# Carrying a decay from the free axis to the partitions: through device memory by DMA instead of by products with ones

## Chip, cores and metric

One core of a Trainium2 chip runs the kernel. The metric is the device time in microseconds of one execution, from the median of several runs. The engines are TensorE (PE, with PEld for its weight loads), VectorE (DVE), ScalarE (ACT), GpSimd (POOL) and SyncE (SP); each works off its own queue in order, and waits on semaphores for the others. Sixteen DMA engines move data for all of them.

## The reference

A gated linear attention over 768 steps, for 4 batches and 8 heads of 48 dimensions, and behind it a two-layer network with a squared ReLU on all 3072 tokens (384 to 2048 to 384):

```python
for t in range(S):                                  # S = 768
    state = alpha[:, :, t, :, None] * state + np.einsum('bhd,bhe->bhde', k[:, :, t], v[:, :, t])
    y[:, :, t] = np.einsum('bhd,bhde->bhe', q[:, :, t], state)
x = y.transpose(0, 2, 1, 3).reshape(B * S, H * D)   # 3072 x 384
h = x @ w_in                                        # 384 x 2048
out = np.maximum(h, 0.0) ** 2 @ w_out               # 2048 x 384
```

Inputs and output are float32; alpha lies between 0.8 and 1, and has one value for each step, head and dimension of k.

## The kernel before

The work is cut into 12 units of 256 tokens, numbered g = 0 to 11: first the four batches' first thirds (0 to 3), then their second (4 to 7), then their last (8 to 11). So unit g + 4 goes on with the state that unit g left. Two tokens lie in one partition (256 tokens on 128 partitions, axis j of size 2).

For each unit these steps follow each other; the names are those of the orders further down:

- load: alpha, k, q, v into RAW (lda, ldk, ldq, ldv). Most go through SP's queue; unit 2's and the weights (win0, win1, wout0, wout1) go through POOL's. Unit 3's alpha is issued only when wout0 has landed (AFTER).
- front: decays. For units 2 to 11 (decays_by_pair) the two tokens of a partition are multiplied (pr, on DVE or POOL), a logarithm is taken (ln, ScalarE), and a product with a triangular matrix of ones sums the logarithms over the partitions (m1i, PE, into psW, L684). Exponentials of it, by ScalarE, give the factors for k (ei, L695, tile EK) and for q (ea, L697, tile EQ). The last row of EQ[:, 1] holds each dimension's total decay over the unit.
- The total decay is needed once more, to multiply the state (sd). The state has its k dimensions on the partitions, two heads at a time: tile SBD is 128 x 384. So the total has to stand as a column over the partitions. The kernel before makes it with four more products of PE, of the logarithms as weights with a 128 x 2 matrix of ones (L687, part of m1i), and ScalarE's exponential of these eight columns into ACM (ec, L700). Units 0 and 1 do the like in functions of their own; units 8 to 11 need none, as nothing follows them.
- scaling of q and k (ekm, eqm on DVE), transposes (tr: by PE for units 0 to 2, by DMA through SP's queue from unit 3), scores (p), mask (mk, tile pm), output (y, which takes the state product of the next unit with it), state (sa, sc, sd on DVE or POOL).
- the network: xe and xt bring the unit's output into the layout for PE, s1 is the first layer in 8 groups, re the ReLU, sq the square, s2 the second layer in 8 groups, oe the copy out of PSUM and out the store.

Every operation is recorded by Program.add with what it reads and writes. Program.schedule then orders all engines' queues ahead of the run, with costs, priorities and a table of shifts written into the program; Program.fill puts products with zeros (L1143, name "fill") into PE's idle time ahead of the first s1; Program.place sets the waits, Program.emit writes the queues. The order in which an engine takes its operations is thus fixed. Two parts of it matter here. POOL's queue, from the weights on, is

    wout0 wout1 sd1 pr3 sd2 vc4 pr5 vc5 pr6 vc7 vc10

and PE's, around unit 3's decays, is

    kv2 m1i3 s2_0_1_0 s2_0_1_1 s2_0_1_2 s2_0_1_3 m1s3 y2

(vc is the cast of v, kv a state product, m1s3 a second product with a triangular matrix, s2_0_1_x the second layer of unit 0.) A tile with a number that repeats is one of a few buffers: EQ, EK and ACM have two, by g % 2.

Of the kernel before, what the change touches and what calls it, by code (L numbers as in the profile page):

```python
# [2 lines left out]

# [3 lines left out]
ALU = mybir.AluOpType  # L7
# [7 lines left out]
class Op:  # L15


    __slots__ = ("alts", "eng", "fn", "cost", "prio", "deps", "idx", "lag", "sem", "start", "end", "pos", "name",
                 "users", "ndeps", "mode", "ready", "land")

    def __init__(self, alts, prio, name):
        self.alts, self.prio, self.name = alts, prio, name
        self.eng = self.fn = self.cost = None
        self.deps = {}
        self.lag = 0
        self.sem = None
        self.users = []
        self.pos = None
        self.mode = ("F", "F")
        self.ready = 0.0  # L30
        self.start = self.end = self.land = None


class Program:

    HOP = 35
    PE_LATENCY = 170
    DMA_FIRST = {"sp": 1300, "act": 1300, "pool": 2000}  # L40
    PACKET = (("win", 172), ("wout", 490), ("ld", 22), ("tr", 18), ("xt", 18), ("out", 125))
    SBUF_ONLY = ("pr", "bk", "aq", "ekm", "eqm", "sq", "sb", "sd")
    BIAS = {"pool": 300}
    DMA_LAST = {"sp": 800, "act": 800, "pool": 1900}
    SWITCH = 95
    HALVED = {"qks": 3, "kqt": 3, "raw": 3, "ek": 3, "eq": 3, "acm": 2, "laf": 2}
    AFFINITY = 2500

    SHIFT = {
# [55 lines left out]
    }  # L105

# [1068 lines left out]
```

## Time and profile before

| | |
|---|---|
| device time, three runs | 174.98, 174.0 and 175.28 us; median 174.98 |
| span of the profiled execution | 174.5 us, 5094 instructions, mean granted TensorE clock 1.000 |
| busy in the span | PE 169.1 us, DVE 121.3, ACT 117.6, POOL 18.8 |
| DMA | 33.36 MB in 74743 packets; queue q1 (SP's) 71.4% of the sixteen engines' span, q0 (POOL's) 12.1% |

The profile is of one execution. Its span, from the first instruction to the last, is 174.5 us; the page gives no other time for that execution, so sums are made against this span, and the runs' median is 0.5 us above it. Lines as L687 are those of the kernel before. An engine that is called busy for 97% need not work at its best: matmuls overlap, and their ends are modelled. A wait has the name of what ended it. "q0" and "q1" are the queues through which POOL's and SP's transfers go; one transfer is split over the DMA engines, and the program counts 16 steps of a semaphore for its landing.

### The profile page before, as it was taken

Reading aid. Unit: us, or ns where it says so; the run is one execution under the profiler, and the core shown is the slowest. Engines: PE = TensorE matmul, PEld = TensorE weight load, DVE = VectorE, ACT = ScalarE, POOL = GpSimd, SP = SyncE. Lnnn points to the kernel's source line nnn. Section 1 sums busy time; section 2 is a strip of 40 time slices with the busy share of each in tenths; the row PEclk is TensorE's granted clock in tenths of the full one; section 3 lists DMA queues with packets and bytes.
Section 4 is the critical chain, followed back from the end, with each engine's and each line's share of the span. In section 5 each row is a group of like instructions: output and inputs, shape, how many; then the busy total and the mean of one; then the engine's idle time right before and its main releaser. Section 6 shows DMA issues by size and latency. Waiting matters only on the chain.

```text
span 174.5 us, 5094 instructions
## 1 busy us (share of the span) xinstructions
PE 169.1 (97%) x2237; PEld 130.5 (75%) x2237; DVE 121.3 (70%) x197; ACT 117.6 (67%) x211; POOL 18.8 (11%) x28
## 2 busy tenths in 40 slices
PE   7989999999999999999999999999999999999994
PEld 2556898856886697777788886778788697688773
DVE  5497799797967869866778966868849726322230
ACT  3848698868869569768768757378668564566440
POOL 3159010022102120000100000000200000000000
DMA  5999999979998999798998897999899690040022
GB/s 139 324 297 190 274 303 216 230 208 280 274 229 125 274 235 188 200 222 151 278 212 211 228 196 180 275 201 251 201 214 208 115 196 4 0 135 4 10 80 90
DMA packets 74743, 33.36 MB, mean 191 GB/s; under 512 B 71649, under 2 KB 71905, under 8 KB 74721
## 3 DMA queue, kind: packets, MB, share of 16 engines
q1 hardware_dynamic: 73184, 28.32, 71.4%
q0 software_dynamic: 1536, 4.72, 12.1%
q8 instruction: 17, 0.28, 0.7%
q14 instruction: 6, 0.04, 0.1%
HBM read 25.17 MB, written 4.72 MB: 171 GB/s over the span
## 4 chain that ended last, share of the span: by engine, by line
PE 56%; DMA 26%; ACT 6%; DVE 4%; SPq 3%; POOL 2%; issue 1%
PE psO L1089 22%; PE psWH L1042 22%; DMA raw<-in_v_dram 9%; DMA wout<-in_moe_w_out_dram 8%; DMA raw<-in_alpha_dram 5%; DMA raw<-in_q_dram 5%; SPq L568 3%; PE psO L1143 2%; POOL raw L568 2%; ACT rr L1050 2%; PE psX L843 2%; PE psX L1012 2%; ACT vbf L742 1%; PE psZ L811 1%; PE psX L832 1%; PE psX L940 1%
## 5 line engine op out<-in xcount | busy, mean ns | idle before, releaser
L1042 PE MATMUL psWH<-xt,win 128*128 128x256 bf16 x576 | 73.9, 275 | 0.5 <-ACT rr L1050 0.2
L1042 PEld LDWEIGHTS psWH<-xt,win 128*128 128x128 bf16 x576 | 65.0, 145 | 6.2 <-DVE rr L1052 1.6
L1089 PE MATMUL psO<-wout,gt 128*128 128x384 bf16 x368 | 68.9, 326 | 0.0
L1050 ACT ACTIVATE rr<-psWH 128x512 bf16<-128x512 f32 x83 | 48.9, 596 | 21.5 <-PE psWH L1042 20.0
L1089 PEld LDWEIGHTS psO<-wout,gt 128*128 128x128 bf16 x368 | 34.8, 98 | 18.3 <-DVE gt L1060 0.2
L1060 DVE TENSOR_TENSOR gt<-rr 128x1024 bf16<-128x1024 bf16 (+1 forms) x47 | 28.4, 608 | 25.1 <-ACT rr L1050 24.5
L951 DVE TENSOR_TENSOR pm<-psX,caus 128x1024 bf16<-128x1024 f32 x12 | 14.6, 1220 | 2.4 <-PE psZ L940 2.1
L951 DVE TENSOR_TENSOR pm<-psZ,caus 128x1024 bf16<-128x1024 f32 x12 | 14.6, 1216 | 1.5 <-PE psZ L940 1.4
L1097 ACT ACTIVATE osb<-psO 128x384 f32<-128x384 f32 x19 | 9.3, 489 | 6.8 <-PE psO L1089 6.3
L971 ACT ACTIVATE xbf<-psX 128x768 bf16<-128x768 f32 x12 | 9.7, 806 | 5.0 <-PE psX L832 4.1
L746 DVE TENSOR_TENSOR qks<-raw,eq 128x384 bf16<-128x384 f32 x18 | 10.3, 605 | 3.0 <-DMA raw<-in_q_dram 3.0
L1143 PE MATMUL psO<-zero 128*128 128x512 bf16 (+1 forms) x37 | 10.5, 417 | 1.3 <-DVE zero L489 1.3
L741 POOL CAST vbf<-raw 128x768 bf16<-128x768 f32 x4 | 3.7, 930 | 71.5 <-DMA raw<-in_v_dram 71.5
L1064 ACT ACTIVATE gt<-rr 128x512 bf16<-128x512 bf16 (+1 forms) x13 | 10.8, 828 | 0.4
L751 DVE TENSOR_TENSOR qks<-raw,ek 128x768 bf16<-128x768 f32 x11 | 10.7, 969 | 0.4 <-ACT ek L663 0.3
L1052 DVE TENSOR_SCALAR rr<-psWH 128x512 bf16<-128x512 f32 x13 | 8.9, 687 | 2.0 <-PE psWH L1042 1.6
L742 ACT ACTIVATE vbf<-raw 128x768 bf16<-128x768 f32 x7 | 5.9, 845 | 3.5 <-DMA raw<-in_v_dram 3.5
L717 ACT ACTIVATE la<-raw 128x384 f32<-128x384 f32 x8 | 4.2, 523 | 5.3 <-DMA raw<-in_alpha_dram 5.2
L1143 PEld LDWEIGHTS psO<-zero 128*128 128x128 bf16 x37 | 3.5, 108 | 4.6 <-issue 1.9
L906 DVE TENSOR_TENSOR smd<-psZ,sbd 128x384 bf16<-128x384 f32 x8 | 4.4, 554 | 3.4 <-PE psX L832 3.4
L675 DVE TENSOR_TENSOR prd<-raw 128x384 f32<-128x384 f32 x7 | 4.0, 569 | 2.9 <-DMA raw<-in_alpha_dram 2.9
L678 ACT ACTIVATE lab<-prd 128x384 bf16<-128x384 f32 x10 | 5.2, 520 | 1.1 <-POOL prd L677 0.6
(115 smaller groups left out, 165.9 us busy)
## 6 DMA issues: line engine op xcount, KB each, us to landing
raw<-in_alpha_dram SPq DMA_DIRECT2D x11, 384.0 KB, 4.2
raw<-in_k_dram SPq DMA_DIRECT2D x11, 384.0 KB, 5.1
raw<-in_q_dram SPq DMA_DIRECT2D x11, 384.0 KB, 4.2
raw<-in_v_dram SPq DMA_DIRECT2D x11, 384.0 KB, 4.8
out_dram<-osb SPq DMA_DIRECT2D x11, 384.0 KB, 4.3
win<-in_moe_w_in_dram POOLq DMA_DIRECT2D x2, 768.0 KB, 9.9
wout<-in_moe_w_out_dram POOLq DMA_DIRECT2D x2, 768.0 KB, 15.2
raw<-in_alpha_dram POOLq DMA_DIRECT2D x1, 384.0 KB, 9.7
```

Of the source, the lines that this page charges most:

```text
L746: add("dve", lambda e, j=j, dst=dst: e.tensor_tensor(dst, RAW[r][:, 2, :, j, :].rearrange("p (n x) d -> p n x d", x=2), EQ[la][:, j].rearr ...
L751: add("dve", lambda e, a=a, E=E: e.tensor_tensor(QKS[qs][:, a, :, :, 0:D], RAW[r][:, 1 + a].rearrange("p h j d -> p j h d"), E[la][:].rear ...
L951: add("dve", lambda e, hf=hf, psT=psT: e.tensor_tensor(PM[pm][:, hf].rearrange("p r n j t -> p (r n) (j t)"), psT[:, :, :].rearrange("p r ...
L971: add("act", lambda e: e.activation(XBF[x2][:], psX[:, :, 0:HD], AF.Copy), act_ns(2 * HD), p0 + 6100, reads=[("ps", "X", 0), ("ps", "X", 1 ...
L1042: ins = pe.matmul(psH[hb][:, i * T:(i + 1) * T], WIN[:, kk, hidden(fj)], mov, start=(kk == 0), stop=(kk == KT - 1))
L1050: add("act", lambda e, hb=hb, rr=rr: e.activation(rr, psH[hb], AF.Relu), act_ns(512), pu + 600, reads=[("ps", "H", hb)], writes=[("rr", rb ...
L1052: alts={"dve": (lambda e, hb=hb, rr=rr: e.tensor_scalar(rr, psH[hb], 0.0, None, ALU.max), dve_ns(512))})
L1060: add("dve", lambda e, dst=dst, sq=sq: e.tensor_tensor(dst, sq, sq, ALU.mult), 148 + k * 267, pu + 1200, reads=[("rr", rb, h) for h in ran ...
L1064: "act": (lambda e, dst=dst, sq=sq: e.activation(dst, sq, AF.Square), act_ns(k * 512))})
L1089: ins = pe.matmul(psS, GT[gt][:, fj, j, :], WOUT[:, fj, :], start=(fj * parts % FT == 0), stop=((fj + 1) * parts % FT == 0))
L1097: add("act", lambda e, j=j, psS=psS: e.activation(OSB[ob][:, j], psS, AF.Copy), act_ns(DM), ps_ + 700, reads=[keyS], writes=[("osb", ob, j ...
L1143: pr.fill(lambda n: lambda pe: pe.matmul(psO[:, 0:n], ZERO[:, 0:128], ZERO[:, 0:n], skip_group_check=True), ((512, 216, 420), (256, 109, 2 ...
```

## The change

For units 2 to 7 (TOTALS_BY_DMA) the four products with ones and ScalarE's ec are left out. In their place POOL issues two transfers for each unit: et writes the last row of EQ[:, 1] (8 heads of 48 numbers) to a small tensor in device memory, LINE, in rows of 64; ec reads LINE back, one number at a time, so that two heads' rows become one column of 128 partitions, four columns in all (512 single float32 numbers, into ACM[:, 0:4]). ec waits until et has landed. LINE's columns 48 to 63 must be zero, so two transfers (zline0, zline1) first write zeros from a new tile NIL; et waits for them. sd multiplies by four columns, each spread over 96, where it took eight, each spread over 48.

The orders of the queues are written as tables, and stand as the planner before had put them, apart from what the change adds or takes: POOL's queue is now

    wout0 wout1 zline0 zline1 sd1 et2 ec2 pr3 et3 ec3 sd2 vc4 et4 ec4 pr5 et5 ec5 vc5 pr6 et6 ec6 et7 ec7 vc7 vc10

DVE has one fill more (znil) among the first, and sd3 stands five operations later, behind bk4 lb4 ekm4 eqm1_4 eqm0_4. SP's queue is the same, and so are the 37 products with zeros. With the tables, place also leaves out an engine's wait for itself where two of its operations only read the same bank of PSUM (ScalarE's ea behind ei, ec behind ea).

```diff
+    TOTALS_BY_DMA = (2, 3, 4, 5, 6, 7)
+    NIL = nc.alloc_sbuf_tensor("nil", [H, 64], FP32)
+    add("dve", fill(NIL[:], 0.0), 100, -2e6, writes=[("nil",)], name="znil")
...
-                if incl and not last:
+                if incl and not last and g not in TOTALS_BY_DMA:
                     for p in range(NPR):
                         ins = pe.matmul(psW[:, HD + 2 * p:HD + 2 * p + 2],
                                         LAB[la][:, 2 * p:2 * p + 2, :].rearrange("p h d -> p (h d)"), ONES2[:],
...
-        if not last:
+        if g in TOTALS_BY_DMA:
+            total = EQ[la][127:128, 1, :].rearrange("o (n d) -> o n d", d=D)
+            add("pool", lambda e: e.dma_start(LINE[la].rearrange("(o n) d -> o n d", o=1)[:, :, 0:D], total), 930, p0 + 5000,
+                reads=[("eq", la, 1)], writes=[("line", la)], name=f"et{g}", dma=f"li{la}", lag=300)
+            add("pool", lambda e: e.dma_start(ACM[la][:, 0:NPR], LINE[la].rearrange("(p x) d -> (x d) p", p=NPR),
+                                             allow_slow_non_contiguous=True), 930, p0 + 5001,
+                reads=[("line", la)], writes=[("acm", la)], name=f"ec{g}", dma=f"ac{la}", lag=600)
+        elif not last:
             add("act", lambda e: e.activation(ACM[la][:], psW[:, HD:HD + H], AF.Exp), act_ns(8), p0 + 520,
                 reads=[("ps", "W")], writes=[("acm", la)], name=f"ec{g}")
...
-            acm = bcast(ACM[la], H, [[1, H], [0, D]])
+            by, acm = hd, bcast(ACM[la], H, [[1, H], [0, D]])
+            if g in TOTALS_BY_DMA:
+                by = lambda ap: ap.rearrange("p (n d) -> p n d", n=NPR)
+                acm = bcast(ACM[la], H, [[1, NPR], [0, 2 * D]])
...
+    LINE = [nc.dram_tensor(f"line{i}", (H, 64), FP32).ap() for i in range(2)]
...
+    for i in range(2):
+        add("pool", lambda e, i=i: e.dma_start(LINE[i], NIL[:]), 930, -4.2e5 + i, reads=[("nil",)], writes=[("line", i)],
+            name=f"zline{i}", dma=f"li{i}", lag=300)
...
-    pr.schedule()
-    pr.fill(lambda n: lambda pe: pe.matmul(psO[:, 0:n], ZERO[:, 0:128], ZERO[:, 0:n], skip_group_check=True),
-            ((512, 216, 420), (256, 109, 250)), min(o.start for o in pr.order["pe"] if o.name.startswith("s1_")), zero, 4600)
+    pr.arrange(TABLES, lambda n: lambda pe: pe.matmul(psO[:, 0:n], ZERO[:, 0:128], ZERO[:, 0:n], skip_group_check=True),
+               zero)
```

And in place(), the waits that are left out:

```diff
-                if d.sem is None and d.eng == o.eng == "pe":
+                if d.sem is None and d.eng == o.eng and (o.eng == "pe" or not raw and d in o.shared):
                     continue
```

More of the change, by code (lines that the diff above doesn't have):

```diff
@@ L15 @@
 class Op:
-    __slots__ = ("alts", "eng", "fn", "cost", "prio", "deps", "idx", "lag", "sem", "start", "end", "pos", "name",
-                 "users", "ndeps", "mode", "ready", "land")
+    __slots__ = ("alts", "eng", "fn", "cost", "prio", "deps", "idx", "lag", "sem", "pos", "name", "mode", "shared")
     def __init__(self, alts, prio, name):
@@ L26, in __init__ @@
         self.sem = None
-        self.users = []
         self.pos = None
         self.mode = ("F", "F")
-        self.ready = 0.0
-        self.start = self.end = self.land = None
+        self.shared = set()
 class Program:
[L38 to L45, printed above, removed]
-    HALVED = {"qks": 3, "kqt": 3, "raw": 3, "ek": 3, "eq": 3, "acm": 2, "laf": 2}
-    AFFINITY = 2500
-    SHIFT = {
[55 rows of a table removed]
-    }
+    HALVED = {"qks": 3, "kqt": 3, "raw": 3, "ek": 3, "eq": 3, "acm": 2, "laf": 2}
     def __init__(self, nc):
@@ L113, in __init__ @@
         self.dma_count = {}
-        self.filler = None
+        self.fills = {}
     def add(self, eng, fn, cost, prio, reads=(), writes=(), name="", dma=None, lag=0, after=(), mode=("F", "F"),
@@ L141, in add @@
                 for r in self.readers.get(k, ()):
-                    op.deps.setdefault(r, False)
+                    if r not in op.deps:
+                        op.deps[r] = False
+                        op.shared.add(r)
         for k in writes:
@@ L149, in add @@
                     op.deps.setdefault(r, False)
+                    op.shared.discard(r)
         for k in reads:
@@ L271, in fill, with arrange @@
-    def fill(self, make, sizes, until, after, cold):
-        new = []
-        t = after.land + self.HOP
-        cold += t
-        for o in self.order["pe"]:
-            while t < until:
-                slow = 2 if t < cold else 1
-                fits = [(n, c) for n, c, gap in sizes if o.start - t > gap + (slow - 1) * c]
-                if not fits:
-                    break
-                n, c = fits[0]
-                f = Op({"pe": (make(n), c)}, 0, "fill")
-                f.idx = len(self.ops)
-                f.eng, f.fn, f.cost = "pe", make(n), c
-                f.start, f.end = t, t + c * slow
-                f.deps = {after: True}
-                self.ops.append(f)
-                new.append(f)
-                t = f.end
-            new.append(o)
-            t = max(t, o.end)
-        for i, o in enumerate(new):
-            o.pos = i
-        self.order["pe"] = new
+    def arrange(self, tables, make, after):
+        named = {o.name: o for o in self.ops}
+        assert len(named) == len(self.ops)
+        self.order = {}
+        for e, text in tables.items():
+            self.order[e] = []
+            for x in text.split():
+                if x[0] == "+":
+                    o = Op({e: (make(int(x[1:])), 0)}, 0, "fill")
+                    o.idx = len(self.ops)
+                    o.deps = {after: True}
+                    self.ops.append(o)
+                else:
+                    o = named.pop(x)
+                o.eng = e
+                o.fn, o.cost = o.alts[e]
+                o.pos = len(self.order[e])
+                self.order[e].append(o)
+        assert not named, sorted(named)
@@ new lines, in sequence @@
+    def sequence(self):
+        done, seq = set(), []
+        at = {e: 0 for e in self.order}
+        while len(seq) < len(self.ops):
+            before = len(seq)
+            for e, ops in self.order.items():
+                while at[e] < len(ops) and all(d in done for d in ops[at[e]].deps):
+                    o = ops[at[e]]
+                    done.add(o)
+                    seq.append(o)
+                    at[e] += 1
+            assert len(seq) > before, {e: ops[at[e]].name for e, ops in self.order.items() if at[e] < len(ops)}
+        return seq
@@ L301, in place @@
         waits = {}
-        seq = sorted(self.ops, key=lambda o: (o.start, o.idx))
+        seq = self.sequence()
+        rank = {o: i for i, o in enumerate(seq)}
         needed = set()
@@ L322, in place @@
             mine = []
-            for d in sorted(want.values(), key=lambda d: -d.start):
+            for d in sorted(want.values(), key=lambda d: -rank[d]):
                 s, p = stream(d), place_of(d)
@@ L351, in emit @@
         stores = {}
-        for o in sorted((o for o in self.ops if o.name.startswith("out")), key=lambda o: o.start):
-            stores.pop(o.sem[0], None)
-            stores[o.sem[0]] = o
+        for o in self.order["sp"]:
+            if o.name.startswith("out"):
+                stores[o.sem[0]] = o
         final = [(self.dma_sems[k], self.value[o]) for k, o in stores.items()]
@@ L496, in bass_gla_recurrent__then__act_relu_squared_kernel @@
         add("dve", fill(LAF[i][:, :, :, D:64].rearrange("p j h d -> p (j h) d"), 0.0), 250, -1e6 - 10,
-            writes=[("laf", i)])
-        add("dve", fill(LAB[i][:, :, D:64], 0.0), 150, -1e6 + 20, writes=[("lab", i)])
+            writes=[("laf", i)], name=f"zla{i}")
+        add("dve", fill(LAB[i][:, :, D:64], 0.0), 150, -1e6 + 20, writes=[("lab", i)], name=f"zlb{i}")
     for i in range(NQKS):
         add("dve", fill(QKS[i][:, :, :, :, D:64].rearrange("p a j h d -> p (a j h) d"), 0.0), 500, -1e6 + 10,
-            writes=[("qks", i, 0), ("qks", i, 1)])
+            writes=[("qks", i, 0), ("qks", i, 1)], name=f"zqk{i}")
     flat = [t[:].rearrange("p a b c -> p (a b c)") for t in (CAUS, CAUS1)]
@@ L504, in bass_gla_recurrent__then__act_relu_squared_kernel @@
                           (flat[0], "caus", 1.0), (flat[1], "caus1", 1.0), (ONES2[:], "ones", 1.0)):
-        add("dve", fill(buf, val), 100, -2.5e6, writes=[(key,)])
-    add("pool", select(LINC[:], ALU.is_ge, 0.0, 0, [[1, 128]], -1), 300, -1e6, reads=[("linc",)], writes=[("linc",)])
-    add("pool", select(LSTR[:], ALU.is_gt, 0.0, 0, [[1, 128]], -1), 300, -1e6, reads=[("lstr",)], writes=[("lstr",)])
-    add("dve", fill(OWN[:], 0.0), 100, -2e6, writes=[("own",)])
-    for part in (OWN[0:64, 0:H:2], OWN[64:128, 1:H:2]):
-        add("dve", fill(part, 1.0), 100, -2e6, reads=[("own",)], writes=[("own",)])
-    zero = add("dve", fill(ZERO[:], 0.0), 300, -3e6, writes=[("zero",)])
+        add("dve", fill(buf, val), 100, -2.5e6, writes=[(key,)], name="z" + key)
+    add("pool", select(LINC[:], ALU.is_ge, 0.0, 0, [[1, 128]], -1), 300, -1e6, reads=[("linc",)], writes=[("linc",)], name="slinc")
+    add("pool", select(LSTR[:], ALU.is_gt, 0.0, 0, [[1, 128]], -1), 300, -1e6, reads=[("lstr",)], writes=[("lstr",)], name="slstr")
+    add("dve", fill(OWN[:], 0.0), 100, -2e6, writes=[("own",)], name="zown")
+    add("dve", fill(NIL[:], 0.0), 100, -2e6, writes=[("nil",)], name="znil")
+    for x, part in enumerate((OWN[0:64, 0:H:2], OWN[64:128, 1:H:2])):
+        add("dve", fill(part, 1.0), 100, -2e6, reads=[("own",)], writes=[("own",)], name=f"zown{x}")
+    zero = add("dve", fill(ZERO[:], 0.0), 300, -3e6, writes=[("zero",)], name="zero")
     add("pool", select(IDENT[:], ALU.not_equal, 1.0, 0, [[-1, 128]], 1), 300, -1e6 + 5, reads=[("ident",)],
-        writes=[("ident",)])
+        writes=[("ident",)], name="sident")
     for c, key in enumerate(("caus", "caus1")):
         add("pool", select(flat[c], ALU.is_ge, 0.0, 128 * c, [[-1, 2], [1, 2], [2, 64]], -2), 400, -1e6 + 7,
-            reads=[(key,)], writes=[(key,)])
+            reads=[(key,)], writes=[(key,)], name="s" + key)
     add("act", lambda e: e.activation(flat[1][0:64], flat[0][0:64], AF.Copy), 400, -1e6 + 8,
-        reads=[("caus",), ("caus1",)], writes=[("caus1",)])
+        reads=[("caus",), ("caus1",)], writes=[("caus1",)], name="xcaus")
     def bcast(t, row, dims):
@@ L691, in m1 @@
             return run
-        add("pe", m1(True), pe_ns(1, HD) + (0 if last else pe_ns(4, 8)), p0 + 300,
+        add("pe", m1(True), pe_ns(1, HD) + (0 if last or g in TOTALS_BY_DMA else pe_ns(4, 8)), p0 + 300,
             reads=[("lab", la), ("linc",), ("ones",)], writes=[("ps", "W")], name=f"m1i{g}")
@@ L911, in state @@
         if not last:
-            acm = bcast(ACM[la], H, [[1, H], [0, D]])
+            by, acm = hd, bcast(ACM[la], H, [[1, H], [0, D]])
+            if g in TOTALS_BY_DMA:
+                by = lambda ap: ap.rearrange("p (n d) -> p n d", n=NPR)
+                acm = bcast(ACM[la], H, [[1, NPR], [0, 2 * D]])
             add("dve", lambda e: e.tensor_tensor(TMP[g % 2][:], ps1, SMD[x2][:], ALU.add), dve_ns(HD),
                 p0 + 3600, reads=[key1, ("smd", x2)], writes=[("tmp", g % 2)], name=f"sc{g}")
-            add("pool", lambda e: e.tensor_tensor(hd(SBD[sw][:]), hd(TMP[g % 2][:]), acm, ALU.mult), pool_ns(HD),
+            add("pool", lambda e: e.tensor_tensor(by(SBD[sw][:]), by(TMP[g % 2][:]), acm, ALU.mult), pool_ns(HD),
                 p0 + 8000, reads=[("tmp", g % 2), ("acm", la)], writes=[("sbd", sw)], name=f"sd{g}",
-                alts={"dve": (lambda e: e.tensor_tensor(hd(SBD[sw][:]), hd(TMP[g % 2][:]), acm, ALU.mult), dve_ns(HD))})
+                alts={"dve": (lambda e: e.tensor_tensor(by(SBD[sw][:]), by(TMP[g % 2][:]), acm, ALU.mult), dve_ns(HD))})
     def scores(g):
```

169 lines of the change are left out of this document (62 added, 107 removed), and 55 rows, old and new, of the table SHIFT.

## The prediction, on record before the changed kernel ran

> **What bounds the kernel now.** I read the page first, then the chain of waits, then the timelines of single engines around the places that the change touches. The page says that TensorE has work almost all the time, while the three engines that the change relieves or loads are far from full:
>
> ```profile
> PE 169.1 (97%) x2237; PEld 130.5 (75%) x2237; DVE 121.3 (70%) x197; ACT 117.6 (67%) x211; POOL 18.8 (11%) x28
> ```
>
> The chain that ended last shows what a busy PE is worth. Up to about 40 us it runs over loads; from there on it is mostly PE pieces that follow each other without a break.
>
> ```profile
> 16.73 13.68 DMA wout<-in_moe_w_out_dram
> ...
> 34.10 5.31 DMA raw<-in_v_dram
> 39.44 0.85 ACT vbf L742
> 40.29 0.14 issue
> 40.42 0.36 PE psX L872 x8
> 40.78 0.51 PE psX L879 x32
> ```
>
> From 117.20 to 172.15 the chain holds PE alone, but for 0.05 us. Between 40 and 117 the start-to-start times of the matmuls in PE's timeline leave only some 1 us of real waits (0.27 at 73.9, 0.16 at 99.4, 0.7 around 115 to 117). So TensorE is the bound after 40 us, and a stall of PE put in before that is hardly ever given back; equally, little less than the PE time that is removed comes off the end.
>
> **What it removes.** Units 2 to 7 lose four products with ones each (L687) and one small exponential each (L700):
>
> ```profile
> L687 PE MATMUL psWH<-ones,lab 128*128 128x2 bf16 x24 | 1.4, 164 | 0.0
> L700 ACT ACTIVATE acm<-psWH 128x8 f32<-128x8 f32 x6 | 1.1, 176 | 0.1
> ```
>
> Busy time overstates the products, since they overlap: in the chain four of them take 0.08 us ("44.19 0.08 PE psWH L687 x4"), 0.10 us with the step to the next. Unit 2's lie ahead of the waits of the first 40 us and save nothing. 5 x 0.10 = 0.5 us off the end. ScalarE loses 6 x 0.18 = 1.06 us, and the table version also drops ScalarE's wait on itself between two readers of one bank of PSUM (14 places, the gap from ei to ea is 0.02 to 0.03 us in the rows). L700 is in no piece of the chain; I take 0.1 us for both, bounds 0 and 1.4.
>
> **What it adds on POOL's queue.** (On DVE there is only one fill more, 0.06 us like the smallest fills before, ahead of 2.9 us in which DVE waits for unit 0's ek: nothing.) Two writes of zeros (zline0, zline1) behind wout1, and for each unit a small store (et) and a scattered load of 512 single elements (ec). All of them, and the waits of ec for et and of et for the zeros, stand in POOL's one in-order queue, and data of its DMAs go through queue q0. The new order is: wout1, zline0, zline1, sd1, et2, ec2, pr3, et3, ec3, sd2, vc4, et4, ec4, pr5, and so on. What is behind ec2 is pr3, and pr3 is what unit 3 waits for. POOL before:
>
> ```profile
> 16.73 1.13 POOL L539 DMA_DIRECT2D wout<-in_moe_w_out_dram  x2
> 22.55 0.83 POOL L915 TENSOR_TENSOR sbd<-tmp,acm 128x384 bf16<-128x384 f32 x1 [4.69 <-DVE tmp L913]
> 35.32 1.00 POOL L677 TENSOR_TENSOR prd<-raw 128x384 f32<-128x384 f32 x1 [11.95 <-DMA raw<-in_alpha_dram]
> ```
>
> POOL sat idle for 12 us here, which looks like room for et2 and ec2 (ea2, their input, ends at 27.35). But et2 must first wait for zline0, and zline0's data queue behind both halves of wout. When those land:
>
> ```profile
> L539 POOL DMA_DIRECT2D wout<-in_moe_w_out_dram x2: 576/578/581, 16.7 to 17.3; - x2
> DMA to landing us min/median/max: 13.7/15.2/16.8
> ```
>
> The second was issued at 17.31 and took 16.8 us: it lands at 34.1. So, step by step:
> - zline0 is seen at about 34.2 (34.1 to 34.7), and et2 issues.
> - et2 to landing. The trace has no small DMA from POOL. Lower bound: the last small stores of SP, 1.5 us. Upper: the first win transfer, issued at 9.37 for 0.94 us, had its first packet only in the window 12.0:12.5 (at its start), 1.7 us after the issue's end. I take that delay, the shortest POOL issue (0.58), and 0.37 us from last data to the waiter (wout0's last packets at 30.05, the SP load that waits for it goes at 30.42): 0.58 + 1.7 + 0.4 = 2.7 us, bounds 1.5 and 3.2. Landed at 36.9.
> - ec2's issue: between 0.58 us (wout) and 0.95 us (a raw load with 1024 rows); 512 pieces are nearer the latter, so 0.87. POOL is free at 37.8.
> - pr3 starts at 37.8 in place of 35.32: 2.45 us late; bounds 34.1 + 1.5 + 0.58 = 36.2 (0.9 late) and 34.7 + 3.2 + 0.95 = 38.9 (3.5 late).
>
> [...]
>
> **Who waits for pr3.** ScalarE's ln3 and, behind it, PE's in-order queue:
>
> ```profile
> 36.35 0.52 ACT L678 ACTIVATE lab<-prd 128x384 bf16<-128x384 f32 x1 [0.63 <-POOL prd L677]
> ...
> 36.34 0.51 PE L811 MATMUL psZ<-vbf,qks 64*128 64x96 bf16 x16
> 36.93 0.34 PE L684 MATMUL psWH<-lab,linc 128*128 128x384 bf16 x1
> ```
>
> PE's L684 at 36.93 (m1i3) starts 0.06 us after ln3 ends; it has no slack, and four groups of the second layer (s2_0_1) that could run are queued behind it. So PE stands still for 2.45 us. Given back: about 0.25 us at 40.42, where y2 waited for vc3, whose load does not move. The loads of later units are issued by SP behind transposes that wait for this same work, so they move along and absorb nothing.
>
> **The later totals.** sd3 to sd7 stand on DVE, in order, and now wait for ec. From the end of ea to sd, in the rows before: unit 4 45.32 to 56.31 (less 1.05 for vc4 on POOL: 9.9), unit 5 56.32 to 65.85 (9.5), unit 6 68.42 to 78.40 (10.0), unit 7 81.68 to 90.76 (9.1); sd3 is moved behind five DVE steps, to about 48, 9.7 after ea3. Two hops cost 2.7 + 0.87 + 1.7 + 0.6 + 0.4 = 6.3 us (0.6 for 32 single elements on each of 16 DMA engines, about 18 ns each, the mean packet of q1 being 71.4% x 174.5 x 16 / 73184 = 27 ns). So they lie hidden with 2.8 to 3.7 us over; if that cover goes, DVE stalls by what is lacking, with the squares and pm behind it. pr5 (52.28) and pr6 (63.07) come more than 2 us after ec4 (50.0) and vc5 (60.8) are through. SP's queue keeps its order; its awaited loads share the DMA engines with the scattered elements, 0.6 to 0.9 us a unit: I take 0.2 in all, bounds 0 and 1.5.
>
> **Sum.** +2.45 - 0.25 - 0.5 - 0.1 + 0.2 = +1.8 us on the profiled span of 174.5: 176.3. The three timed runs have a median of 174.98, 0.5 above that span; I carry the 0.5 along: 176.8 us.
>
> **Rivals.**
> 1. *Small POOL transfers starve behind SP's loads.* For: win's first packets came just as SP's earlier loads ran dry.
>
> ```profile
> q1 hardware_dynamic: 422, 0.16, 116.0%
> ...
> q0 software_dynamic: 26, 0.05, 73.4%
> q1 hardware_dynamic: 181, 0.06, 47.2%
> ```
>
> The first line is the window 11.5:12.0 (no q0 at all), the others 12.0:12.5. Against: in 30:35 both queues moved data. Then et2 lands only as the loads thin out near 38.6, pr3 comes at 39.5, 4.2 late, and later totals use up their 2.8 us too: 174.98 + 4.2 - 0.65 = 178.5, up to 181.
> 2. *TensorE loses its clock in the stall.* In this trace it starts slow: nine 512-column matmuls in 4.02 us (447 ns each) against four in 0.81 us later, until about 5.9 us, 4.6 us after its first. If the stall costs a second such start, half of 4.6 goes: 176.8 + 2.3 = 179.1. For: the kernel keeps PE fed with zeros at the start. Against: nothing but gaps up to 0.36 us is seen afterwards, so the trace does not show when the clock falls.
>
> [...]
>
> 3. *The wait is hidden, not slower.* If zline0's few rows do not have to wait for the slowest engine's share of wout, et2 and ec2 run in POOL's idle time before 35.3, m1i3 waits for the alpha load as before, and what is left is -0.5 - 0.1: 174.4. It decides if zline0 lands before about 32. Against: q0 serves win, raw and wout in the order of issue (their landings follow it), and the code counts 16 steps for one landing, the slowest engine's among them.
> 4. *ScalarE's relief counts in full.* On top of 3, 1.06 us of L700 and some 0.3 us of dropped waits come off the end: 173.0. Against: no L700 in the chain.
>
> **Chances.** Forecast 0.55 (own range 175.7 to 177.8: the stall 1.3 to 3.4); rival 1 0.20, rival 2 0.07, rival 3 0.13, rival 4 0.05. One per cent, 1.75 us, is about what a measurement of this kernel can tell from no change; it lies just under the forecast, so I give 0.30 of its 0.55 to slower and 0.25 to the same. Slower 0.30 + 0.20 + 0.07 = 0.57, same 0.25 + 0.13 = 0.38, faster 0.05. For 8 in 10 the range goes from 174.4 (rival 3) to 180.4 (most of rival 1).
>
> **What would show it.** Right: POOL's prd of unit 3 starts near 37.8 with et2's landing as what ended its wait; PE has one gap of 2 to 3 us ahead of unit 3's L684; every sd on DVE starts without waiting for the acm DMA; PE spans after 45 us are 1.5 to 2 us later than before, by the same amount up to the end. Wrong: pr3 near 35.3 (rival 3), a gap over 3.5 us or matmuls at 200 ns and more behind it (1 and 2), DVE waits on acm, or et's landings far from 2.7 us.

## The result, and the profile after

The changed kernel takes 182.31 us (median of 6 runs, 181.79 to 183.59); the kernel before, run beside it, takes 175.13 us (6 runs, 174.0 to 175.81). The ratio is 1.0414, 95% interval 1.0376 to 1.0451: slower, by 7.2 us. The forecast of 176.8 us had the sign; its range, up to 180.4, did not reach the time. The profiled execution of after took 182.4 us around a span of 180.7, so 1.7 us lie outside the span. Ratios, here and below, leave out disturbed runs, which the medians contain, so a ratio can differ from the quotient of two medians.

From the page after, the busy times and the granted clock by slices (each 4.5 us long, 9 is full speed):

```profile
PE 171.6 (95%) x2213; PEld 130.3 (72%) x2213; DVE 120.5 (67%) x198; ACT 116.0 (64%) x205; POOL 27.0 (15%) x42
PEclk9999999995899999999999999999999999999999
```

PE has 24 instructions less than before and is busy 2.5 us longer. The slices at 40.7 to 49.7 us say why: the clock is at half in the first and at 0.8 in the second. In shorter windows it stands at half from 39.9 to 46.7 us, and at full speed before and after. The mean granted clock over this execution is 0.981; four of the six runs have that mean, the other two 0.99.

The chain that ended last (start, duration, what), around 17 to 40 us and around 62 to 70 us:

```profile
17.81 16.33 DMA line<-nil
34.18 0.50 issue
34.70 3.34 DMA line<-eq
38.04 0.28 issue
...
39.13 1.02 POOL prd L568
40.17 0.53 ACT lab L569
...
41.25 5.18 PE psO L990 x16
...
62.98 4.97 DMA line<-eq
...
69.02 0.85 POOL vbf L639
```

Before, the chain was PE alone from 40.4 to 66.8 us and, but for 0.05 us, from 117.2 to 172.2. Up to 40 us it ran over loads, and so it did between 66.8 and 117.2, where six loads took 27.0 us of it; three of them:

```profile
68.20 5.09 DMA raw<-in_v_dram
...
84.31 4.31 DMA raw<-in_alpha_dram
...
109.39 4.93 DMA raw<-in_alpha_dram
```

Now, up to unit 3's decays, it goes exactly the way that the change laid: the zeros (16.3 us behind wout), et2, ec2's issue on POOL, pr3, ln3, m1i3 (L575 in this kernel, L684 before). Between a landing and POOL's next transfer stand 0.50 and 0.28 us in which, by the profile, nothing is waited for. The second part shows the same hop again, for unit 5: et5 takes 4.97 us, and vc5, behind ec5 in POOL's queue, is what PE waits for (0.45 us) at 70.0.

POOL's timeline at the first place (start, duration, and in brackets the idle time before and what ended it):

```profile
34.70 0.56 POOL L592 DMA_DIRECT2D line<-eq  x1 [11.26 <-ACT kqt L681]
38.32 0.79 POOL L594 DMA_DIRECT2D acm<-line  x1 [3.06 <-DMA line<-eq]
```

pr3 starts at 39.13 in place of 35.32: 3.8 us late. In the first line the bracket names the last event that the profile saw; the wait that really ended there is the one for the zeros, which landed at 34.1 to 34.3.

PE's timeline behind that:

```profile
40.75 0.50 PE L575 MATMUL psWH<-lab,linc 128*128 128x384 bf16 x1 [3.81 <-ACT lab L569]
41.13 5.30 PE L990 MATMUL psO<-wout,gt 128*128 128x384 bf16 x16
```

PE stands for 3.8 us, and the 16 matmuls of the second layer that follow take 324 ns each (5.18 / 16 in the chain), where the same shape takes 163 ns otherwise: 1.30 us for 8 of them further down in this chain. That is 16 x 0.161 = 2.6 us more. Set against the trace of before, unit 3's m1i is 3.8 us late, the next output (y2) 6.3 us, the scores of unit 3 and the outputs of units 4 to 7 6.2 to 7.0 us, and the last instruction 6.2. By the trace, then, the loss is complete at 46.7 us: 3.8 of stall, and 2.5 that follow it and are put down to the clock here; e2 tests that. The other 1.0 of the 7.2 us is the execution of before that was profiled: its span of 174.5 and the same 1.7 around it make 176.2, 1.1 above the median of before.

The windows of the stretch, after and then before (stretch, length, busy us and count of PE, PEld, DVE, ACT, POOL, granted clock, DMA share, GB/s):

```profile
36.00:45.00 9.00, 5.18 (x34) 2.43 (x32) 4.32 (x7) 2.50 (x5) 2.33 (x3) 0.72 0.92 239
45.00:60.00 15.00, 14.96 (x181) 10.77 (x179) 10.89 (x16) 10.58 (x20) 5.10 (x6) 0.94 0.69 124
```

```profile
36.00:45.00 9.00, 8.75 (x128) 5.86 (x127) 8.00 (x14) 6.35 (x14) 1.79 (x2) 1.00 0.96 265
45.00:60.00 15.00, 15.00 (x221) 11.44 (x220) 11.91 (x21) 12.04 (x24) 1.95 (x3) 1.00 1.04 220
```

In the first 9 us there are 34 matmuls instead of 128. In the stretch behind them transfers run at 124 GB/s where they ran at 220: the loads have moved along with the work, as the prediction had it, and give nothing back.

The waits (who <- for what: total us, times, longest), and what the transfers cost (count, KB each, median us from issue to landing):

```profile
POOL acm L594 <- DMA line<-eq: 20.7, 6, 4.7
...
DVE sbd L818 <- DMA acm<-line: 1.8, 2, 1.1
```

```profile
line<-eq POOLq DMA_DIRECT2D x6, 1.5 KB, 3.6
acm<-line POOLq DMA_DIRECT2D x6, 2.0 KB, 5.2
```

POOL spends 20.7 us in waits of ec for et, with everything behind ec in its queue waiting too, and DVE's sd does wait for totals twice.

### The profile page after: what moved, and what is told of

It is laid out like the page before. It is cut to its first block, busy times and chain, and to the rows that moved or that the text cites. A ratio compares the mean times of both kernels' runs of the same rounds, so it can differ in the third digit from the quotient of the medians.

```text
span 180.7 us, 5062 instructions
## 1 busy us (share of the span) xinstructions
PE 171.6 (95%) x2213; PEld 130.3 (72%) x2213; DVE 120.5 (67%) x198; ACT 116.0 (64%) x205; POOL 27.0 (15%) x42
## 3 DMA queue, kind: packets, MB, share of 16 engines
q1 hardware_dynamic: 73184, 28.32, 70.8%
## 4 chain that ended last, share of the span: by engine, by line
PE 67%; DMA 18%; POOL 5%; DVE 4%; ACT 3%; issue 2%; POOLq 0%; SPq 0%
PE psO L990 27%; PE psWH L943 27%; DMA line<-nil 9%; DMA line<-eq 5%; DMA raw<-in_alpha_dram 2%; PE psO L1047 2%; DMA raw<-in_q_dram 2%; POOL raw L459 2%; PE psX L741 2%; PE psX L841 2%; PE psX L913 1%; PE psX L730 1%; PE psZ L709 1%; PE psWH L575 1%; DVE qks L511 1%
## 5 line engine op out<-in xcount | busy, mean ns | idle before, releaser
L990 PE MATMUL psO<-wout,gt 128*128 128x384 bf16 x368 | 71.5, 335 | 0.0
L990 PEld LDWEIGHTS psO<-wout,gt 128*128 128x128 bf16 x368 | 35.7, 100 | 20.1 <-issue 2.4
L644 DVE TENSOR_TENSOR qks<-raw,eq 128x384 bf16<-128x384 f32 x18 | 9.4, 553 | 3.9 <-DMA raw<-in_q_dram 3.9
L602 DVE TENSOR_TENSOR ek<-ek,raw 128x384 f32<-128x384 f32 x10 | 5.5, 554 | 4.2 <-ACT ek L586 4.2
L592 POOL DMA_DIRECT2D line<-eq x6 | 3.2, 534 | 32.4 <-ACT eq L588 21.1
L594 POOL DMA_DIRECT2D acm<-line x6 | 4.8, 793 | 20.7 <-DMA line<-eq 20.7
```

Source lines behind the costliest of these rows:

```text
L644: add("dve", lambda e, j=j, dst=dst: e.tensor_tensor(dst, RAW[r][:, 2, :, j, :].rearrange("p (n x) d -> p n x d", x=2), EQ[la][:, j].rearr ...
L990: ins = pe.matmul(psS, GT[gt][:, fj, j, :], WOUT[:, fj, :], start=(fj * parts % FT == 0), stop=((fj + 1) * parts % FT == 0))
```

## The experiments

Three questions were put: what the stall ahead of unit 3's decays costs, and how much of it is the clock; what the later transfers cost behind it; and what the removal of the products brings. In the expectations theory 1 puts the whole loss at m1i3, and theory 2, with its letters, puts a part of it at the later transfers. Each ratio is to the kernel before on the same chip in the same session. That kernel's median lay between 174.97 and 176.84 us by session, so ratios are compared here and not times; a difference of two ratios mostly goes over two sessions.

### The stall and the clock

**e1_pr3_first.** pr3 goes ahead of et2 and ec2 in POOL's queue.

```diff
-        ... wout0 wout1 zline0 zline1 sd1 et2
-        ec2 pr3 et3 ec3 sd2 vc4 ...
+        ... wout0 wout1 zline0 zline1 sd1 pr3
+        et2 ec2 et3 ec3 sd2 vc4 ...
```

> POOL's order alone is changed: pr3 stands ahead of et2 and ec2, nothing else. Theory 1 (the queue): pr3 is late only because et2's wait for the zeros and ec2's wait for et2 stand ahead of it in POOL's queue, and PE's stall of 3.8 us ahead of unit 3's L575, with the slow matmuls behind it, follows from that. Then pr3 starts at 35.3 again, PE has no gap over 0.4 us before 45, the granted clock is 1.000 in all stages, and the time is 182.3 - 3.8 - 2.6 = about 175.6 us (174.6 to 176.6). Theory 2 (the transfers themselves): the scattered loads and the late totals of units 3 to 7 cost time wherever they stand; then at least 2 us of the 7 stay and the time is 177.5 or more.

Measured: 178.68 us, ratio 1.0152 (1.0092 to 1.0213). The stall is gone (m1i3 at 37.70), and the granted clock of the profiled execution is 1.000; in one of the other three it is 0.99, and no trace is kept that shows why. 2.6 of the 4.1% go away by moving one instruction past two. But theory 1's return to the old time does not come. New small waits stand on PE: 0.36 us at 51.0 (for a transpose by DMA), 0.47 at 54.9 (for a mask of DVE), 0.64 at 56.6 (unit 5's decays: pr5 behind ec4), 0.35 at 65.7 (vc5 behind ec5) and 0.38 at 76.8 (for a cast behind a load). POOL's part in the third:

```profile
54.11 0.81 POOL L594 DMA_DIRECT2D acm<-line  x1 [4.60 <-DMA line<-eq]
54.94 1.01 POOL L568 TENSOR_TENSOR prd<-raw 128x384 f32<-128x384 f32 x1
```

A second limit lay behind the first. In the trace of after little of it can be seen, since everything there had been pushed 6 us later already.

**e2_warm.** 16 products with zeros into the same bank keep PE busy in the stall; the wait for pr3 stays.

```diff
+            add("pe", warm, ..., writes=[("ps", "W")], name="warm")   # 16 x pe.matmul(psW, ZERO[:, 0:128], ZERO[:])
-        ... kv2 m1i3 s2_0_1_0 ...
+        ... kv2 warm m1i3 s2_0_1_0 ...
```

> The changed kernel with 16 products of zeros (128 x 512, into the bank that unit 3's L575 writes next) put ahead of unit 3's L575 in PE's queue: 16 x 0.216 = 3.5 us of work inside the stall of 3.8 us, which stays. Theory 1a: the matmuls of 324 ns behind the stall are TensorE's lower clock, lost because PE stood still. Then the granted clock stays at 1.000 in the stages 36 to 60, the 16 matmuls behind L575 take 163 ns each, and the time falls by what the clock cost, 2.6 us or a little more, to 179.0 to 179.9 us. Rival: they are slow because of something that the late start collides with (loads, weights, the stores); then filling PE changes nothing and the time stays at 182.3 or rises.

Measured: 181.39 us, ratio 1.0296 (1.0234 to 1.0358), clock 1.000. PE's timeline:

```profile
41.55 0.34 PE L575 MATMUL psWH<-lab,linc 128*128 128x384 bf16 x1 [1.33 <-ACT lab L569]
41.93 2.77 PE L996 MATMUL psO<-wout,gt 128*128 128x384 bf16 x16
```

The wait that is left, 1.33 us, costs no clock: 2.77 us for the 16 matmuls that took 5.30. m1i3 starts even later than in after (41.55), and the kernel is still faster. So the clock is worth 1.0414 - 1.0296 = 1.2% (about 0.7 either way), some 2.1 us. From here to e1 it is 1.0296 - 1.0152 = 1.4%, some 2.5 us, for the stall itself. That is less than the 3.8 us of the trace: without the stall, waits appear that it had hidden.

**e10_warm5.** The same with 5 products, to leave a break of 2.7 to 3.0 us and see whether the clock falls after that.

```diff
-                for x in range(16):
+                for x in range(5):
```

> The changed kernel with 5 products of zeros ahead of unit 3's L575 in place of 16: 1.1 us of work, so that PE stands still for about 2.7 to 3.0 us in one piece instead of 3.9 (none of work) or 1.5 (with 16). If the clock is lost only after a break longer than this, the granted clock stays at 1.000 and the time is that of the run with 16; if a break of this length is enough, the matmuls behind it take 324 ns again and the time is that of the changed kernel.

```profile
41.71 0.34 PE L575 MATMUL psWH<-lab,linc 128*128 128x384 bf16 x1 [3.50 <-ACT lab L569]
42.09 4.45 PE L996 MATMUL psO<-wout,gt 128*128 128x384 bf16 x16
```

Measured: 181.61 us (2 runs), ratio 1.0352 (1.0272 to 1.0432), clock 0.991. Unit 3's decays came at 41.71 us in this execution, against 40.75 in after, so the break was 3.5 us and not under 3, and the clock fell all the same. It is inconclusive on the point it was made for: a break of 1.33 us keeps the clock, 3.5 and 3.8 us lose it, and what lies between is open. But it shows something else. The granted clock is at half only from 42.9 to 46.3 us: it falls 1.2 us after PE has taken up work again (L575 takes 0.34 us here, 0.50 in after), and the slow stretch is 3.4 us long. In after it is 6.8 us long, and began while PE stood still, 3.0 us after its last product. So in these two executions the length of the break alone does not set when the clock falls (4.7 us after PE's last product in e10, 3.0 in after), nor for how long (3.4 and 6.8 us).

**e4_zeros_early.** The zeros are written ahead of the weights, so that et2 does not wait for them.

```diff
-        ... scaus1 vc0 win0 win1 ... wout0 wout1 zline0 zline1 sd1 et2
+        ... scaus1 zline0 zline1 vc0 win0 win1 ... wout0 wout1 sd1 et2
```

> The two writes of zeros stand ahead of win in POOL's queue; et2, ec2, pr3 stand as in the changed kernel. So et2 needs to wait only for ea2 (27.4). If q0 serves its transfers in the order of issue, et2's rows still queue behind wout and land at about 34.2, but nothing of a new transfer's delay is left to pay: ec2 goes at about 34.5 and pr3 at about 35.4, and the time is near 175.6 us (174.6 to 176.6). If et2's row could overtake wout, it lands near 31 and the time is the same. If instead the hop of 3.3 us is paid after wout in any case (the delay starts when the ring runs empty), pr3 comes at 38 to 39, PE stands still again, and the time is 179 to 182.

Measured: 178.22 us, ratio 1.0136 (1.0058 to 1.0214), clock 1.000. POOL's timeline:

```profile
27.72 0.57 POOL L592 DMA_DIRECT2D line<-eq  x1 [4.14 <-ACT eq L588]
34.88 0.80 POOL L594 DMA_DIRECT2D acm<-line  x1 [6.59 <-DMA line<-eq]
```

et2 goes out 7 us earlier and lands at 34.6, 6.9 us after its issue. It stands in q0 behind wout, as the zeros did in after, and wout's second half lands at 34.4. pr3 then starts at 35.77, and 0.30 us of PE's wait remains. This shows the prediction's step "zeros behind both halves of wout": in both kernels the small transfer issued behind wout lands within 0.3 us of it. The ratio is about that of e1, so two ways of taking the stall away leave the same rest.

### The later transfers

**e5_interleaved.** POOL's queue is ordered so that every vc, pr and sd stands between an et and its ec, or ahead of both.

```diff
-        et2 ec2 et3 ec3 sd2 vc4 et4 ec4 pr5 et5 ec5 vc5 pr6 et6 ec6 et7 ec7 vc7 vc10     (as in e1)
+        et2 ec2 et3 vc4 ec3 et4 sd2 pr5 ec4 et5 vc5 ec5 pr6 et6 ec6 et7 vc7 ec7 vc10
```

> The changed kernel with POOL's order as sd1 pr3 et2 ec2 et3 vc4 ec3 et4 sd2 pr5 ec4 et5 vc5 ec5 pr6 et6 ec6 et7 vc7 ec7: POOL's own work stands in the time in which it would wait for et's landing, and no pr or vc stands behind a wait for a landing. With pr3 first alone 1.8 us of the loss stayed, and the trace of that run has gaps of 0.5 to 0.8 us on PE ahead of unit 5's decays (pr5 behind ec4), unit 4's output (vc5 behind ec5) and others. Theory 1b (POOL's queue again): these go, and the time is that of before less up to 0.5 us for the products, a ratio of 0.995 to 1.005. Theory 2b (the totals come too late for DVE, or the transfers slow SP's loads): ec4 to ec7 now go even later, DVE waits longer for acm, and the ratio is 1.01 or more.

Measured: 176.85 us against 175.51, ratio 1.0064 (1.002 to 1.0108). So 0.9% (about 0.75 either way) of e1's 1.5% was work queued behind ec on POOL. In two of the ten executions (not in the ratio) the mean granted clock is 0.99, while it is 0.999 or more in all 31 of before; no trace of those two is kept. What is left is under 1%, and the waits of DVE for the totals had grown (1.6 us in e1):

```profile
DVE sbd L818 <- DMA acm<-line: 3.9, 4, 1.6
```

**e9_late_multiply.** e5, with sd3 to sd7 moved behind the masks of their unit on DVE, so that none waits for a total.

```diff
-        bk5 sd4 lb5 ekm5 eqm1_5 eqm0_5 mk0_4 mk1_4 re3_2 ...
+        bk5 lb5 ekm5 eqm1_5 eqm0_5 mk0_4 mk1_4 sd4 re3_2 ...     (sd3, sd5, sd6, sd7 likewise)
```

> As the interleaved order of POOL, and on DVE sd3 to sd7 moved behind the masks (mk) that follow them, 5 to 9 us later; their results are wanted only four units later. In the interleaved run DVE waited 3.9 us in four places for acm, and 0.64% over before stayed. Theory 2c: this rest is the late totals. Then no sd waits for acm, and the ratio falls to 0.995 to 1.002 (products saved, nothing else left). Rival: the rest is something else (the moved order of POOL, other loads); the waits go and the ratio stays at 1.005 or more.

Measured: 177.06 us against 175.23, ratio 1.0097 (1.006 to 1.0134). The wait of 3.9 us is gone from the trace, and nothing is gained. Either late totals (2c) are not what is left and DVE had that time to spare, or the later sd costs as much.

**e6_totals_alone, e7_copies, e8_moved** take POOL's computing out of the question: pr3, pr5, pr6 go to DVE and vc4, vc5, vc7 to ScalarE. e6 has the totals by DMA; in e7 the products and exponentials make the totals and the transfers go to a tile that nobody reads; e8 has no transfers at all.

```diff
-        wout0 wout1 zline0 zline1 sd1 et2 ec2 pr3 et3 ec3 sd2 vc4 et4 ec4 pr5 ...     POOL, after
+        wout0 wout1 zline0 zline1 sd1 et2 ec2 et3 ec3 sd2 et4 ec4 et5 ec5 ...         POOL, e6 (dc for ec in e7)
+        wout0 wout1 sd1 sd2 vc10                                                       POOL, e8
```

> The changed kernel with pr3, pr5, pr6 moved to DVE and vc4, vc5, vc7 to ScalarE, so that behind the totals POOL's queue holds nothing that PE waits for but sd2 and, much later, vc10. ec's go as early as et's landing lets them. Theory 1b: all of the loss beyond the moved work's own price is gone; beside the control with the products and the same moved work the ratio is 0.3% lower (the products) or the same. Theory 2b: what is left of 1.5% is here too, as waits of DVE for acm or as later loads.

> As the one before (pr and vc moved off POOL), but the totals are again made by products and ScalarE's exponentials, and the two transfers of each unit go to a tile that nobody reads: all DMA traffic of the change, and no engine but POOL that waits for it. If the transfers themselves slow SP's loads, this run is slower than the control by that, 0.2 us by my prediction (0 to 1.5). If not, it equals the control within 0.3 us, and what separates it from the run before is the late totals against the saved products.

> The control: products and exponentials as before, no transfers, pr3, pr5, pr6 on DVE, vc4, vc5, vc7 on ScalarE, sd3 five places later. DVE has 1.7 us more and ScalarE 2.5 us more, neither of them full; some 0 to 1 us slower than before, by where these stand.

Measured: e6 176.67, ratio 1.006 (1.0023 to 1.0097); e7 175.86, 1.0032 (0.9998 to 1.0067); e8 176.11, 1.0038 (1.0 to 1.0077). e7 and e8 differ by the twelve transfers and the zeros (with NIL's fill) alone, and not in time, to about 0.5%: the traffic costs nothing that shows. With only sd2 and vc10 of POOL's work behind an ec, the full change (e6) is 0.2% above the control e8, within the intervals.

**f_units4to7.** The change for units 4 to 7 only; units 2 and 3 keep the products, so nothing that comes early waits for the zeros behind wout. sd3 stands in its old place.

```diff
-    TOTALS_BY_DMA = (2, 3, 4, 5, 6, 7)
+    TOTALS_BY_DMA = (4, 5, 6, 7)
```

> The change for units 4 to 7 alone; units 2 and 3 have the products and the exponential again, and POOL's order is otherwise that of the changed kernel (pr5 behind ec4, vc5 behind ec5, vc7 behind ec7). Theory 1 and 1b: no stall at unit 3's decays and no lost clock; what the later units cost by themselves stays: 0.5 us for vc5 behind ec5 and some for late totals, a ratio of 1.003 to 1.012. If the later units cost nothing the ratio is 1.000 or under; if they cost all of the rest that pr3 first left, 1.015.

Measured: 176.03 us against 175.23, ratio 1.0049 (1.0015 to 1.0083), clock 1.000. The large loss belongs to units 2 and 3; the other four, by themselves, still bring a small loss and no gain.

### What the removal brings

**e3_tables_only.** The products and the exponentials stay; only the orders as tables and ScalarE's dropped waits for itself are new.

```diff
-    TOTALS_BY_DMA = (2, 3, 4, 5, 6, 7)
+    TOTALS_BY_DMA = ()
```

> The products with ones and ScalarE's exponentials are back for units 2 to 7, with no transfer of totals and no fill of NIL; every queue has the order of the kernel before. What is left of the change is the waits of an engine for itself between readers of one PSUM bank. My prediction gave them 0.1 us (bounds 0 and 0.3): 174.8 to 175.2 us beside 175.1 before. A rival, that the dropped waits or the tables cost or bring something of their own, would show as more than 0.5 us either way.

Measured: 176.43 us, ratio 1.0015 (0.9971 to 1.006): no difference.

**e11_no_totals.** Products, exponentials and transfers are all left out, sd multiplies by what units 0 and 1 left in ACM, and POOL's order is that of before. It shows what the removal could bring if the totals came free.

```diff
         if g in TOTALS_BY_DMA:
-            add("pool", ... name=f"et{g}" ...)
-            add("pool", ... name=f"ec{g}" ...)
+            pass
```

> For units 2 to 7 no total decay is made at all: no products with ones, no exponential, no transfers (this leaves out part of the computation: the state of these units is multiplied by the totals that units 0 and 1 left in ACM). POOL's order is that of before. This is the removal alone. By my sum it is worth 0.5 + 0.1 us: a ratio of 0.995 to 0.998. Rival: the 0.5 us of PE do not come off the end, since what PE waits for between 40 and 117 us are loads and transposes whose times do not move; then the ratio is 1.000 to 1.003.

Measured: 175.84 us against 174.97, ratio 1.0046 (1.0013 to 1.0079). PE's busy time fell by 0.7 us (168.4 for 169.1), and the kernel is no faster. Unit 3's output starts at 53.16 us, 0.3 earlier than before, but behind it PE waits, and unit 5's decays start 0.3 us later than before, where they started at 54.45:

```profile
54.76 0.34 PE L574 MATMUL psWH<-lab,linc 128*128 128x384 bf16 x1 [0.56 <-ACT lab L568]
```

They wait for pr5 on POOL, and that for the load of unit 5's alpha, until 53.13 us where it was 52.28 before. The chain between 48 and 65 us runs over transfers too:

```profile
48.90 6.30 DMA kqt<-qks
...
55.21 3.61 DMA raw<-in_q_dram
...
58.84 4.64 DMA raw<-in_alpha_dram
...
63.55 1.02 POOL prd L567
```

Here a transpose by DMA, then two loads, then unit 6's pr set the pace, and PE's saved time turns into waiting. That fits the missing gain; it does not explain the 0.46% of loss, for which the later place of sd3 (which e11 shares with after, and e8 too) is a candidate that was not tried by itself.

**e12_unread.** e9 with ec going to a tile that nobody reads; sd multiplies by the stale ACM as in e11. All transfers and waits of POOL stay, no one needs a total.

```diff
-            add("pool", lambda e: e.dma_start(ACM[la][:, 0:NPR], LINE[la]...
+            add("pool", lambda e: e.dma_start(DUM[la][:], LINE[la]...
```

> The run with the late multiplications again (same orders on every engine, same zeros, et and ec), but ec writes to a tile that nobody reads and sd uses what stands in ACM (the totals of units 0 and 1, so part of the computation is left out). It differs from that run by no wait for a total, and from the run without any total by the transfers, by POOL's waits for et's landing and by the moved order. If the traffic and POOL's time are what is left, the ratio is again 1.006 to 1.010; if the landing of the totals is, it falls to that of the run without totals.

Measured: 176.59 us against 174.97, ratio 1.0091 (1.0057 to 1.0125), the same as e9's 1.0097. So the totals' landing costs nothing once sd is late; e12 is 0.45% above e11 (about 0.5 either way), which the transfers, POOL's waits, the changed order and the late sd share, and which is not clearly different from nothing.

**Together.** Of the 4.1%, taken off in this order: 1.2 the lost clock, 1.4 the stall, 0.9 the work behind later ecs on POOL, 0.6 a rest. The first three are known to 0.7 to 0.9 either way. The rest is no larger than what e8 (no transfers, 0.4) and e11 (no totals, 0.5) lose, so nothing in it can be laid to the transfers with certainty, and its cause stays open. No version is faster than the kernel before: the nearest, e3 and e7, are the same within their intervals.

## Why the prediction was wrong, point by point

- **Where the loss arises: right.** Zeros behind wout, et2 behind the zeros, pr3 behind ec2, one break on PE ahead of m1i3 that nothing gives back: all of it stands in the chain, at the places named. The zeros landed at 34.14 and et2 was issued at 34.70, within the forecast (34.2, 34.1 to 34.7).
- **Size of the hop: too small.** 2.7 us from et2's issue to ec2's, bounds 1.5 and 3.2, with 0.4 us in it from the last data to the waiter; measured 3.34 to the landing and 0.28 more until POOL went on, 3.62 together. et2 itself was issued 0.5 us later than the 34.2 of the sum. ec2's issue was 0.79 (0.87). pr3 came 3.8 us late in place of 2.45, above the upper bound of 3.5. This term is short by 1.4 us: 0.9 in the hop, 0.5 ahead of it.
- **The clock: the step that failed.** The sum had +1.8 us on the span, and 6.2 were measured. Of the 4.4 that lack, 1.4 are the stall, and 2.5 the clock, which the sum put at nothing. It stood as rival 2, priced well (2.3 us; the trace has 2.5, e2 has 2.1) and given 0.07. The price was near in part by luck: it took a slow spell of 4.6 us, and PE worked 6.0 us at half rate (40.75 to 46.7). That the clock would stand the sum's 2.45 us of break was not shown by any row of before: PE's longest wait there, behind its first, is 0.56 us (at 9.22, for DVE's qks; the prediction has 0.36). The stall came to 3.8 us by the 0.9 and 0.5 us above, without any starving. The two terms were treated as separate cases, though the second hangs on the size of the first: in the runs a break of 1.33 us kept the clock (e2), 3.5 and 3.8 us lost it (e10, after), and the rate was half (324 ns for 163 in after); but the fall came 3.0 us after PE's last product in after, and in e10 only when PE was 1.2 us back at work. As nothing in before shows what break the clock stands, the range should have carried stall and clock together, 3.5 + 2.3 us at its upper end before anything else.
- **Later totals: the cover was not there.** 6.3 us for two hops, "hidden with 2.8 to 3.7 over". Measured: et 2.9 to 5.0 us, ec 2.9 to 5.9, and 0.28 us or more between. The 0.6 us for the elements, at 18 ns each, was an estimate below q1's mean of 27 ns a packet; no run shows that term (ec shows as 16 packets, 41 ns each in the median). DVE waited 1.8 us for two totals. That cost nothing that could be shown (e9, e12). What did cost, 0.9% in e1, is what the prediction dismissed where it let pr5 and pr6 come more than 2 us after ec4 and vc5: with hops of this length pr5 and vc5 come out late behind ec4 and ec5. In after, most of it lies hidden behind the first stall, which had moved everything else by 6 us.
- **-0.5 us for the products, -0.1 for ScalarE: not there.** e11 has no totals at all and is not faster. The rule of the first part, that PE time removed comes off the end, did not hold for these five places. It read the chain of before as mostly PE from 40 us on, but between 66.8 and 117.2 us six loads hold 27.0 us of it. PE has hardly a gap there (busy 14.7 to 15.0 us of each 15 between 60 and 120), so loads and PE's work are two paths of nearly the same length, and shortening one alone gains little; the wait in e11's trace fits that, and no run tests it by itself.
- **+0.2 us of traffic: nothing measurable** (e7 against e8). The 512 single elements show as 16 packets of 128 bytes, 41 ns each in the median, where the prediction counted 32 single elements on each of 16 engines.
- **Rival 1** was not needed: the first packets of et came 0.9 to 2.1 us after the end of its issue, those of ec 0.8 to 2.4, around the 1.7 read from win. It gave about the right lateness for pr3 (4.2) for the wrong reason. Rivals 3 and 4 fall with the chain.
- **+0.5 us from span to time:** 1.7 in the profiled execution of after. The 0.5 compared one execution's span with other executions' median.

In after, of et's 2.9 to 5.0 us from issue to landing (median 3.6), 0.9 to 2.1 lie between the end of the issue and the first packet, and 0.3 to 1.1 between the last packet and the landing; of ec's 2.9 to 5.9 (median 5.2) it is 0.8 to 2.4 and 0.4 to 2.1.

## What to carry to other kernels

A wait in an in-order queue costs whatever stands behind it, so order the queue by what others wait for: moving one multiply past two small transfers took back 2.6 of 4.1% (e1). A break of the bounding engine has to be priced together with its clock: here 3.8 us of stall brought 6.8 us at half clock with it, worth 2.1 to 2.5 us. Where the traces at hand don't show what break the clock stands, both belong into the range as one case. Work taken off the bounding engine need not be a gain where loads are as long as its work: e11's removal of 0.7 us brought nothing.

## What the runs showed of the hardware

- TensorE's clock survived a break of 1.33 us (e2) and fell to half with breaks of 3.5 (e10) and 3.8 us (after), in after at 324 ns in place of 163 for a 128 x 384 product. The slow stretch was 6.8 us long in after (39.9 to 46.7) and 3.4 in e10 (42.9 to 46.3), where it began 1.2 us behind the break.
- Beside a busy q1 (70.8% of the sixteen engines' span in after), 1.5 KB from POOL to device memory took 2.9 to 5.0 us from issue to landing, 2 KB of single elements back 2.9 to 5.9; POOL went on 0.28 and 0.50 us after a landing (after's chain).
- Small transfers on q0 landed only with the weights ahead of them: behind 1.5 MB of weights, 2 KB of zeros took 16.3 us (after; landed at 34.14, the weights at 33.99), and 1.5 KB issued 10 us behind the weights 6.9 us (e4; 34.6 us, the weights 34.4).
